# A linear-attention and MLP kernel: chunk 0's output transfers put behind a transposing transfer on the same queue

## The chip, the cores and the metric

The kernel runs on one core of a Trainium2 chip. The core has five instruction streams that run beside each other: TensorE (PE, matrix products; its weight loads are listed as PEld), VectorE (DVE), ScalarE (ACT), GpSimd (POOL) and SyncE (SP). In this kernel SP does no arithmetic; it only begins transfers, one after the other, in the order of its program. POOL begins the loads that change the type from f32 to bf16. Sixteen DMA engines carry the transfers of both.

The metric is device time in microseconds (us), lower is better. Before the change the median of three runs is 286.52 us (286.44 to 286.90).

## The reference

Linear attention (a positive feature map, no softmax) feeds a two-layer MLP whose activation is `h - tanh(h)`. The weight names begin with `moe_`, but there is no routing.

```python
# q, k, v: (8 batches, 8 heads, 576 positions, 64)
phi = lambda x: np.where(x > 0, x, np.exp(x) - 1.0) + 1.0
q_p, k_p = phi(q), phi(k)
kv  = np.einsum('bhsd,bhse->bhde', k_p, v)
z   = np.sum(k_p, axis=2)
num = np.einsum('bhsd,bhde->bhse', q_p, kv)
den = np.einsum('bhsd,bhd->bhs', q_p, z)[..., None] + 1e-06
x   = (num / den).transpose(0, 2, 1, 3).reshape(4608, 512)
h   = x @ w_in                 # 512 x 2048
out = (h - np.tanh(h)) @ w_out # 2048 x 512, f32 result
```

## The kernel before, in words

**Tiles and stages.** The attention is worked per batch `b` (eight batches of 576 rows). The MLP is worked per chunk `c` (nine chunks of 512 rows), so a chunk straddles batches: chunk 2 (rows 1024 to 1535) is made of rows of batches 1 and 2. For each chunk, layer 1 is 64 products (line 430) into PSUM (the accumulators that PE writes), with tanh on ACT (L436, L441) and the subtraction on DVE (L437, L442). Layer 2 is 64 products (L451), whose four results are copied to an SBUF tile `osb` by ACT (L460) and sent to DRAM by SP (L471). Each `osb` is sent as two transfers of 64 rows, so a chunk makes eight.

**What a batch needs.** POOL begins the loads `load_k`, `load_q`, `load_v` (L92); for batch `b` they fill the tiles `kraw`, `qraw` and `v`. ACT and DVE make phi(k) and phi(q) (L136 to L138, tiles `kp`, `qp`). phi(q) has to be turned round (`qT`). For batches 0 and 1 PE does this; from batch 2 on one transfer begun by SP does it (`a_qT_dma`, L155). `qT` then feeds the products of line 337 (denominators, batches 0 to 2) and of lines 273 and 281 (numerators). For batch 2 the reciprocal denominators go to DRAM (`ds`, L366, four small transfers) and come back spread over the partitions (`rdb`, L369, two large ones). Line 401 multiplies the numerators by `rdb` into `xT`, the input of layer 1. Batches 3 and later scale phi(q) before it is turned round and need no `rdb`.

**The order of the work is written by hand.** For each chunk there are lists `s1[fi]` and `s2[s]` of extra work: `s1[fi]` runs after step `fi` of layer 1, `s2[s]` after step `s` of layer 2. Nothing reorders them later: each engine has its instructions in the order in which the Python code issues them. The places that matter here:

- Chunk 0, the last steps of layer 2: steps 12 to 15 finish the four accumulators and call `evac`, each followed at once on SP by its two output transfers. After step 15 the list `s2[15]` runs: the second half of phi(q) of batch 2 (`rest2(qs[1])`), its transposing transfer `a_qT_dma(2)`, and the DVE part of phi(k) of batch 2.
- Chunk 1, `s1[0]`: POOL copies v of batch 2 (`a_vp`, L199), then runs `gate` (L447), a copy of one element of `qT` that lets POOL go on only when the transposing transfer of batch 2 has landed, and then begins the loads of batch 3 (L92). `s1[12]`: the denominators of batch 2 and the trip through `ds` and `rdb`.
- Chunk 1, layer 2: phi of batch 3 (`s2[2]` to `s2[8]`), the numerators of batch 2 and the scaling of line 401 (`s2[12]`), a small product `q_zb` for batch 3 (L221, `s2[14]`). Chunk 2 then starts at line 430 with the columns of `xT` that line 401 wrote.

**Buffers.** `osb` has five buffers, `kraw` and `qraw` one each, `v` and `qT` two. Transfers of SP carry one of eight completion counters in turn, so a transfer also waits until the transfer eight before it has landed.

Of the kernel before, what the change touches and what calls it, by code (L numbers as in the profile page):

```python
# [18 lines left out]
def kernel(  # L19
# [9 lines left out]
    nc = tc.nc  # L29
    B, H, S, D = q.shape  # L30
# [6 lines left out]
    J = S // 64  # L37
# [57 lines left out]
    def load_k(b):  # L95
        k_t[b] = kpool.tile([128, 2, 2, J, D], BF16, name="kraw")
        load(b, k_t[b], k, b == 0)

    def load_q(b):
        q_t[b] = kpool.tile([128, 2, 2, J, D], BF16, name="qraw")  # L100
        load(b, q_t[b], q, b == 0)

    def load_v(b):
        load(b, v_b[b % 2][:, 0:2], v, b < 2)
# [39 lines left out]
    def a_kphi(b, i):  # L144
        phi(b, k_t, kp_t, "kp", i)

    def a_qphi(b, i):
        phi(b, q_t, qp_t, "qp", i)

    def new_qT(b):  # L150
        qT_t[b] = work.tile([128, 2, J, 2, 64], BF16, name="qT")

    def a_qT_dma(b):
        new_qT(b)
        nc.sync.dma_start_transpose(  # L155
            out=qT_t[b].rearrange("p i j g t -> p (i j) (g t)"),
            in_=qp_t[b].rearrange("p i j h d -> p (i j h d)"))
# [29 lines left out]
    def a_kv(b, b0):  # L187

        kz_t[b], vt = kz_c[b % 2], v_b[b % 2]
        kv_mm(b, lambda rs, h, i, j: vt[rs, h:3:2 - h, i, j, :],  # L190
              lambda cs, hg, i: ps_all[cs, b0 + hg, 128 * i:128 * i + 128].rearrange("p (a e) -> p a e", a=2))

    def a_kz(b, b0):
        ps = ps_all[:, b0:b0 + 2, 0:256].rearrange("p g (i e) -> p g i e", i=2)
        nc.vector.tensor_mul(kz_t[b][:, :, :, 64:96], ps[:, :, :, 64:96], mask)
        nc.vector.tensor_copy(kz_t[b][:, :, :, 0:64], ps[:, :, :, 0:64])
# [4 lines left out]
    def kv_cols_mm(b, b0, o):  # L201
        kz_t[b] = kz_c[b % 2]
        kv_mm(b, lambda rs, h, i, j: vp[rs, i, j, h, :],
              lambda cs, hg, i: ps_all[cs, b0 + hg, o + 66 * i:o + 66 * i + 66])
# [64 lines left out]
    def num_mm(b, i, bank_of):  # L269

        kz, qT = kz_t[b], qT_t[b]
        for rs, cs, h, hg in quads():
            nc.tensor.matmul(ps_all[cs, bank_of(h), :].rearrange("p (j t) -> p j t", j=8), kz[rs, hg, i, 0:64],  # L273
                             qT[rs, i, 0:8, hg, :], start=True, stop=True)

    def rest_mm(b, b0, o):

        kz, qT = kz_t[b], qT_t[b]
        for i in range(2):
            for rs, cs, h, hg in quads():  # L280
                nc.tensor.matmul(ps_all[cs, b0 + h, 64 * i + o:64 * i + o + 64], kz[rs, hg, i, 0:64],
                                 qT[rs, i, 8, hg, :], start=True, stop=True)
        return [ps_all[:, b0 + h, o:o + 128].rearrange("p (i t) -> p i t", i=2) for h in range(2)]
# [37 lines left out]
    def scale_rest(b, pss):  # L321
        rdb = rdb_t[b]
        for h, ps in enumerate(pss):
            nc.vector.tensor_mul(
                xT[:, 2 * h:2 * h + 2, S * b + 512:S * b + 576].rearrange("p a (t c) -> p a t c", t=4),
                ps.rearrange("p a (t c) -> p a t c", t=4), rdb[:, 2 * h:2 * h + 2])
# [83 lines left out]
    def new_ns(b):  # L410

        return rpool.tile([128, NP, J, 64], F32, name="ns", tag="rdb")

    def a_spread_pe(b, pairs):

        for n, p in enumerate(pairs):
            for t in range(4):
                r = slice(32 * t, 32 * t + 32)
                nc.tensor.matmul(ps_all[:, 4 + t, 128 * n:128 * n + 128], sel3[r, p].rearrange("p h e -> p (h e)"),
                                 rden_t[b][r, 0:128], start=True, stop=True)  # L420

    def a_scale(b, p, ns, n):
        nc.vector.tensor_mul(
            xT[:, p, S * b:S * b + 512].rearrange("p (j t c) -> p t j c", j=8, t=4),
            ns[:, p, 0:8].rearrange("p j (t c) -> p t j c", t=4),
            ps_all[:, 4:8, 128 * n:128 * n + 128].rearrange("p t (j c) -> p t j c", c=16))
# [22 lines left out]
    def l2mm(gT, o, i, f0, f1):  # L449
        for fi in range(f0, f1):  # L450
            nc.tensor.matmul(o, gT[:, fi, i * 128:(i + 1) * 128], w_out_sb[:, fi, :],  # L451
                             start=(fi == 0), stop=(fi == NF - 1))

    def evac(c, i, o, f0=0, f1=None):
        f1 = DM if f1 is None else f1
        osb = opool.tile([128, DM], F32, name="osb")
        if f0:
            nc.vector.tensor_copy(osb[:, f0:f1], o[:, f0:f1])  # L458
        else:
            nc.scalar.copy(osb[:, f0:f1], o[:, f0:f1])  # L460

        if c == NC - 1 and i == 3:
            nc.sync.dma_start(
                out=out[(B - 1) * S:, f0:f1].rearrange("(p j) m -> p j m", j=J)[:, J - 2:J],
                in_=osb[:, f0:f1])
            return
        for half in range(2):
            b, j = divmod(2 * (4 * c + i) + half, J)
            cuts = [f0, 256, f1] if c == 3 else [f0, f1]
            for a0, a1 in zip(cuts, cuts[1:]):  # L470
                nc.sync.dma_start(  # L471
                    out=out[b * S:(b + 1) * S, a0:a1].rearrange("(p j) m -> p j m", j=J)[:, j, :],
                    in_=osb[64 * half:64 * half + 64, a0:a1])


    nc.vector.memset(zero, 0.0)  # L476
# [20 lines left out]
    for h in range(2):  # L497
        for hg in range(2):
            for i in range(2):
                m = 4 * hg + 2 * h + i  # L500
# [76 lines left out]
    for c in range(NC):  # L577
# [3 lines left out]
        s2 = {i: [] for i in range(16)}  # L581
        if c == 0:
            sub = {}

            def spread1():
                a_spread_pe(1, range(NP))
                for p in range(NP):
                    a_scale(1, p, sub["ns"], p)

            def kv1():  # L590
                a_kv(1, 4)
                pss = rest_mm(0, 4, 256)
                a_kz(1, 4)
                scale_rest(0, pss)

            def num1():
                ns = sub["ns"] = new_ns(1)
                for i in (1, 0):
                    b0 = 4 + 2 * i
                    num_mm(1, i, lambda h: b0 + h)  # L600
                    nc.scalar.copy(ns[:, i::2, 0:8, :].rearrange("p a j t -> p a (j t)"), ps_all[:, b0:b0 + 2, :])

            s1[11].append(lambda: a_kphi(1, 0))
            s1[13].append(lambda: a_kphi(1, 1))
            s2[3].append(lambda: a_qphi(1, 0))
            s2[4].append(lambda: (a_qphi(1, 1), load_q(2), load_k(2), load_v(2)))
            s2[0].append(prepare)
            s2[8].append(lambda: (a_qT_pe(1, 0, Banks([4, 5])), a_qT_pe(1, 1, Banks([6, 7])), kv1()))
            s2[9].append(lambda: (a_den(1, 4), num1(), spread_rest(1), a_split(1)))
            s2[12].append(spread1)  # L610

            qs, ks = [], []

            def exp2(pieces, src, store, name, i):
                pieces.append(phi_pieces(2, src, store, name, i))
                pieces[i][0]()

            def rest2(f):
                f[1]()
                f[2]()  # L620

            def k2(i):
                ks.append(phi_pieces(2, k_t, kp_t, "kp", i))
                ks[i][1]()

            s2[11].append(lambda: exp2(qs, q_t, qp_t, "qp", 0))
            s2[13].append(lambda: (rest2(qs[0]), exp2(qs, q_t, qp_t, "qp", 1)))
            s2[15].append(lambda: (rest2(qs[1]), a_qT_dma(2), k2(0), k2(1)))
        elif n1 < B:
            if c == 1:  # L630
                def kv2():
                    kv_cols_mm(2, 6, 0)
                    pss = rest_mm(1, 6, 256)
                    kz_copy(2, 6, 0)
                    scale_rest(1, pss)

                s1[8].append(kv2)
            if n1 < QS:
                s1[12].append(lambda: (a_den(n1, 6), a_spread(n1)))
            else:  # L640
                if c == 2:
                    s1[2].append(lambda: (q_den(n1, 0, 0), q_den(n1, 0, 1)))
                e = 2 * (c == 2)
                s1[3 + e].append(lambda: q_den(n1, 1, 0))
                s1[5 + e].append(lambda: q_den(n1, 1, 1))
                s1[7 + e].append(lambda: q_scale(n1))
            m = 12 if c == 1 else 9
            s2[m].append(lambda: a_num(n1, n2 if n2 < B else 0))
            if n2 < B:
                s2[m + 2].append(lambda: (q_zb(n2, 4 if c == 1 else 7), q_prod(n2)))  # L650
                if c > 1:
                    s2[15].append(lambda: (q_den(n2, 0, 0), q_den(n2, 0, 1)))
# [46 lines left out]
        for s in range(16):  # L699
# [14 lines left out]
            if c == 0 and g == 2:  # L714
                for n in (2 * i, 2 * i + 1):
                    f = 8 + 2 * (n // 4)
# [37 lines left out]
```

## Time and profile before

| what | value |
|---|---|
| median of three runs | 286.52 us (286.44 to 286.90) |
| profiled execution, its own time | 285.73 us |
| its span | 284.0 us |
| PE busy | 274.4 us (97%) |
| DVE busy | 175.9 us (62%) |
| ACT busy | 145.1 us (51%) |
| POOL busy | 77.4 us (27%) |
| granted TensorE clock | 1.0 throughout |
| bytes moved by DMA | 33.12 MB, mean 117 GB/s |
| output transfers of 128 KB | 62, median 2.5 us to landing |
| transposing transfers | 6, median 4.7 us to landing |

The span is shorter than the time of the same execution by 1.73 us, which lies around it. All moments in the text count from the start of the span. "A <- B" in a list of waits says that A stood idle until B ended. In the list of DMA queues, q0 holds what POOL begins and q1 what SP begins. The DMA share of a window is the mean over the sixteen engines of the time that packets took, and can be above 1.

### The profile page before, as it was taken

What the parts mean: (1) busy time and instruction counts of PE and PEld (TensorE: products, weight loads), DVE (VectorE), ACT (ScalarE), POOL (GpSimd) and SP (SyncE); (2) the same over time, 40 slices, a digit from 0 to 9 for tenths busy, and PEclk for the clock granted to TensorE, in tenths of its full rate; (3) what the DMA queues carried; (4) which work ended last, traced back from release to release, by engine and by line L of the source; (5) the groups of instructions that cost most, each with busy time, mean ns of one, the idle gap of its engine ahead of it and who ended that gap; (6) DMA issues with size and microseconds to landing.
All of it is one profiled execution on the core that took longest, in us unless ns stands there. A gap on an engine that the chain in (4) does not pass through costs nothing.

```text
span 284.0 us, 5064 instructions
## 1 busy us (share of the span) xinstructions
PE 274.4 (97%) x2056; PEld 131.5 (46%) x2084; DVE 175.9 (62%) x283; ACT 145.1 (51%) x176; POOL 77.4 (27%) x69
## 2 busy tenths in 40 slices
PE   7889999999999999999999999999999999999995
PEld 2564454444434454445444444444444444444443
DVE  5859967984679773976397648764770267006600
ACT  3648546945345663666355736663551355126411
POOL 8743030330180536143605360505050000000000
PEclk9999999999999999999999999999999999999999
DMA  6999999869996299147912793151106210230032
GB/s 100 203 206 210 206 206 209 180 109 201 237 254 117 46 187 214 40 79 129 231 47 54 123 228 82 33 120 43 37 12 124 60 37 2 53 79 17 2 73 74
DMA packets 38743, 33.12 MB, mean 117 GB/s; under 512 B 16160, under 2 KB 34624, under 8 KB 38592
## 3 DMA queue, kind: packets, MB, share of 16 engines
q0 software_dynamic: 17504, 18.35, 39.7%
q1 hardware_dynamic: 21216, 14.45, 21.7%
q8 instruction: 16, 0.26, 0.3%
q14 instruction: 7, 0.06, 0.1%
HBM read 38.14 MB, written 9.46 MB: 168 GB/s over the span
## 4 chain that ended last, share of the span: by engine, by line
PE 67%; DMA 20%; issue 4%; DVE 4%; POOL 3%; ACT 2%; SPq 0%; DVEq 0%; POOLq 0%
PE ps_all L430 34%; PE ps_all L451 30%; DMA qraw<-in_q_dram 9%; DMA v<-in_v_dram 8%; DMA out_dram<-osb 2%; DVE qp L138 1%; PE ps_all L273 1%; POOL vp L199 1%; PE ps_all L184 1%; DVE xT L401 1%; ACT e L136 1%; POOL kraw L92 1%; ACT osb L460 1%; DVE r L137 1%; POOL w_out_sb L112 1%
## 5 line engine op out<-in xcount | busy, mean ns | idle before, releaser
L451 PE MATMUL ps_all<-w_out_sb,gT 128*128 128x512 bf16 x543 | 122.4, 379 | 1.6 <-issue 1.1
L430 PE MATMUL ps_all<-xT,w_in_sb 128*128 128x512 bf16 x550 | 122.3, 379 | 1.1 <-DVE xT L401 0.4
L437 DVE TENSOR_TENSOR gT<-ps_all,th 128x1024 bf16<-128x1024 f32 x64 | 77.7, 1217 | 46.1 <-ACT th L436 46.1
L436 ACT ACTIVATE th<-ps_all 128x1024 f32<-128x1024 f32 x64 | 65.7, 1026 | 47.5 <-PE ps_all L430 45.5
L430 PEld LDWEIGHTS <-w_in_sb 128*128 128x128 bf16 x560 | 54.6, 98 | 66.5 <-issue 1.3
L451 PEld LDWEIGHTS <-gT 128*128 128x128 bf16 x560 | 53.9, 98 | 63.4 <-issue 0.2
L460 ACT COPY osb<-ps_all 128x512 f32<-128x512 f32 (+1 forms) x36 | 20.7, 582 | 53.8 <-PE ps_all L451 37.5
L245 POOL TENSOR_TENSOR qp<-qp,rd 128x1152 bf16<-128x1152 bf16 x10 | 21.0, 2118 | 39.8 <-issue 23.7
L231 POOL TENSOR_TENSOR pr<-qp,zb 128x1152 f32<-128x1152 bf16 x10 | 23.5, 2361 | 19.5 <-ACT zb L224 17.0
L136 ACT ACTIVATE e<-qraw 128x1152 bf16<-128x1152 bf16 x16 | 18.5, 1162 | 9.1 <-DMA qraw<-in_q_dram 9.1
L236 DVE TENSOR_REDUCE dn<-pr 128x9 f32<-128x576 f32 x20 | 14.5, 746 | 12.2 <-POOL pr L231 12.2
L136 ACT ACTIVATE e<-kraw 128x1152 bf16<-128x1152 bf16 x15 | 17.5, 1167 | 2.3 <-DMA kraw<-in_k_dram 2.3
L138 DVE TENSOR_TENSOR qp<-e,r 128x1152 bf16<-128x1152 bf16 x16 | 12.1, 758 | 5.0 <-ACT e L136 4.0
L138 DVE TENSOR_TENSOR kp<-e,r 128x1152 bf16<-128x1152 bf16 x15 | 11.7, 783 | 5.0 <-ACT e L136 4.3
L92 POOL DMA_DIRECT2D kraw<-in_k_dram x7 | 5.4, 772 | 27.5 <-ACT e L136 14.1
L442 DVE TENSOR_TENSOR gT<-ps_all,th 128x512 bf16<-128x512 f32 x16 | 10.3, 686 | 2.4 <-ACT th L441 1.7
L441 ACT ACTIVATE th<-ps_all 128x512 f32<-128x512 f32 x16 | 9.2, 598 | 4.9 <-PE ps_all L676 3.7
L92 POOL DMA_DIRECT2D qraw<-in_q_dram x7 | 5.2, 744 | 19.5 <-DVE r L137 12.2
L523 PE MATMUL ps_all<-zero 128*128 128x512 bf16 x31 | 8.7, 433 | 1.3 <-DVE zero L476 1.2
L199 DVE COPY vp<-v 128x1152 bf16<-128x1152 bf16 x10 | 5.2, 524 | 4.0 <-DMA v<-in_v_dram 4.0
L137 DVE TENSOR_SCALAR r<-qraw 128x1152 bf16<-128x1152 bf16 x16 | 7.4, 460 | 0.5 <-DMA qraw<-in_q_dram 0.5
L458 DVE COPY osb<-ps_all 128x128 f32<-128x128 f32 x1 | 0.3, 292 | 11.6 <-DMA out_dram<-osb 11.6
(105 smaller groups left out, 140.5 us busy)
## 6 DMA issues: line engine op xcount, KB each, us to landing
out_dram<-osb SPq DMA_DIRECT2D x62, 128.0 KB, 2.5
kraw<-in_k_dram POOLq DMA_DIRECT2D x7, 576.0 KB, 7.5
qraw<-in_q_dram POOLq DMA_DIRECT2D x7, 576.0 KB, 8.5
v<-in_v_dram POOLq DMA_DIRECT2D x6, 576.0 KB, 11.5
w_in_sb<-in_moe_w_in_dram POOLq DMA_DIRECT2D x3, 512.0 KB, 13.0
w_out_sb<-in_moe_w_out_dram POOLq DMA_DIRECT2D x3, 512.0 KB, 17.3
v<-in_v_dram POOLq DMA_DIRECT2D x4, 288.0 KB, 12.4
rdb<-ds SPq DMA_DIRECT2D x2, 576.0 KB
```

Source lines behind the costliest of these rows:

```text
L92: nc.gpsimd.dma_start(out=t.rearrange("q h i j d -> q (h i) (j d)"), in_=x.rearrange("(n q) x -> q n x", n=4))
L136: return (lambda: nc.scalar.activation(e, x, AF.Exp), lambda: nc.vector.tensor_scalar(r, x, 0.0, 1.0, ALU.max, ALU.add), lambda: nc.vector ...
L138: lambda: nc.vector.tensor_tensor(y, e, r, ALU.min))
L231: nc.gpsimd.tensor_mul(pr_t[b][:, i].rearrange("p j h d -> p j (h d)"), qp_t[b][:, i].rearrange("p j h d -> p j (h d)"), zb_t[b][:, i].uns ...
L236: nc.vector.tensor_reduce(dn_t[b][:, i, :, h], pr_t[b][:, i, :, h, :], mybir.AxisListType.X, ALU.add)
L245: nc.gpsimd.tensor_mul(x, x, rd[:, i].unsqueeze(2).to_broadcast([128, J * 2, D]))
L430: nc.tensor.matmul(h, w_in_sb[:, p, fi * 128:(fi + 1) * 128], xT[:, p, c * 512:(c + 1) * 512], start=(n == 0), stop=(n == NP - 1))
L436: nc.scalar.activation(th, h, AF.Tanh)
L437: nc.vector.tensor_sub(gT[:, fi:fi + 2, :], h, th)
L442: nc.vector.tensor_sub(gT[:, fi, :], h, th)
L451: nc.tensor.matmul(o, gT[:, fi, i * 128:(i + 1) * 128], w_out_sb[:, fi, :], start=(fi == 0), stop=(fi == NF - 1))
L460: nc.scalar.copy(osb[:, f0:f1], o[:, f0:f1])
```

## The change

For chunk 0 `evac` no longer begins its two output transfers; it puts a function that does so into a list `later`. The list is run in `s2[15]` of chunk 0, right behind `a_qT_dma(2)`. The eight transfers themselves (addresses, sizes, order among each other) are the same, and so is everything for chunks 1 to 8. On SP the row of eight output transfers and the transposing transfer of batch 2 change places; the order of the instructions on PE, DVE, ACT and POOL stays as it was. The lines of the changed file lie up to nine higher.

```diff
+    later = []
+
     def evac(c, i, o, f0=0, f1=None):
...
-        for half in range(2):
-            b, j = divmod(2 * (4 * c + i) + half, J)
-            cuts = [f0, 256, f1] if c == 3 else [f0, f1]
-            for a0, a1 in zip(cuts, cuts[1:]):
-                nc.sync.dma_start(
-                    out=out[b * S:(b + 1) * S, a0:a1].rearrange("(p j) m -> p j m", j=J)[:, j, :],
-                    in_=osb[64 * half:64 * half + 64, a0:a1])
+
+        def store():
+            for half in range(2):
+                b, j = divmod(2 * (4 * c + i) + half, J)
+                cuts = [f0, 256, f1] if c == 3 else [f0, f1]
+                for a0, a1 in zip(cuts, cuts[1:]):
+                    nc.sync.dma_start(
+                        out=out[b * S:(b + 1) * S, a0:a1].rearrange("(p j) m -> p j m", j=J)[:, j, :],
+                        in_=osb[64 * half:64 * half + 64, a0:a1])
+
+        if c == 0:
+            later.append(store)
+        else:
+            store()
...
-            s2[15].append(lambda: (rest2(qs[1]), a_qT_dma(2), k2(0), k2(1)))
+            s2[15].append(lambda: (rest2(qs[1]), a_qT_dma(2), [f() for f in later], k2(0), k2(1)))
```

## The prediction

> **What bounds the kernel now.** I read the page's engine shares first, then the chain that ended last, then the instructions of SP, PE and DVE in order of time around the places the change touches, and last the DMA queues window by window.
>
> ```profile
> PE 274.4 (97%) x2056; PEld 131.5 (46%) x2084; DVE 175.9 (62%) x283; ACT 145.1 (51%) x176; POOL 77.4 (27%) x69
> ```
>
> PE is busy nearly always, so only moments at which PE stands still can be won. Those that the change can reach are in this stretch of the chain (start us, length us, what):
>
> ```profile
> 52.34 2.77 POOL vp L199 x2
> 55.11 5.83 issue
> 60.97 0.09 POOL g L447
> ...
> 61.55 0.49 POOL kraw L92
> ...
> 63.01 10.38 DMA v<-in_v_dram
> 73.50 0.46 DVE vp L199
> ...
> 78.98 2.50 DVE xT L401 x4
> 81.52 6.85 PE ps_all L430 x31
> ```
>
> Read it backwards. PE's layer 1 of chunk 2 waited at 81.52 for DVE's scaling; DVE was late because it got v of batch 3 only at 73.50 and from there worked without a gap (5.48 us to line 401); v was late because its load was begun at 63.01; and that because POOL stood at the gate until 60.97. From 81.52 to 266.92 the chain is PE alone. What held the gate is on SP and in the waits:
>
> ```profile
> 50.77 5.24 SPq L471 DMA_DIRECT2D out_dram<-osb  x8
> 56.12 2.92 SPq L155 DMA_TRANSPOSE qT<-qp  x1
> 63.83 1.39 SPq L366 DMA_DIRECT2D ds<-rden  x4
> 70.17 1.12 SPq L369 DMA_DIRECT2D rdb<-ds  x2
> ```
>
> ```profile
> POOL g L447 <- DMA qT<-qp: 5.9, 1, 5.9
> ```
>
> The second half of phi(q) was ready at 51.03 (DVE, line 138, 50.27 + 0.76), but the transposing transfer stood behind eight output transfers until 56.12. What PE lost by this is read from its rows between 77 and 82 us:
>
> ```profile
> 77.66 0.81 PE L451 MATMUL ps_all<-w_out_sb,gT 128*128 128x512 bf16 x3
> 78.72 0.28 PE L221 MATMUL ps_all<-ident,zr 128*128 128x128 bf16 x2 [0.25 <-DVE zr L212]
> 78.84 1.03 PE L451 MATMUL ps_all<-w_out_sb,gT 128*128 128x512 bf16 x4
> 79.73 0.38 PE L430 MATMUL ps_all<-xT,w_in_sb 128*128 128x512 bf16 x1
> 80.32 1.02 PE L430 MATMUL ps_all<-xT,w_in_sb 128*128 128x512 bf16 x4 [0.22 <-DVE xT L401]
> 81.52 0.81 PE L430 MATMUL ps_all<-xT,w_in_sb 128*128 128x512 bf16 x3 [0.17 <-DVE xT L401]
> ```
>
> A product lasts 0.38 us but the next starts 0.21 after it: four take 1.02, and (1.02 - 0.38) / 3 = 0.21. The last of the three at 77.66 starts at 78.09, so L221 could start at 78.30 and starts at 78.72: 0.42 lost. The second L430 could start at 79.94 and starts at 80.32: 0.38. The fifth starts at 80.96; the sixth could follow at 81.17 and starts at 81.52: 0.35. Together 1.15 us; that is all there is to win here.
>
> **The change part by part.**
>
> *The transposing transfer goes ahead of eight output transfers on SP.* SP was free at 50.67 (the `rdb` transfers of line 316 end there), phi(q) is ready at 51.03, the tile's former readers (line 281 for batch 0) were done at 40.6, and its completion counter is now shared with a transfer of line 316 of batch 0, long landed. So it starts at about 51.1, 5.0 us earlier. In the trace it took 4.85 us from its start to the gate (56.12 to 60.97); I take that again, since the load of v of batch 2 leaves the DMA engines at about 52 and the first data came 1.4 us after the start. The gate opens at 51.1 + 4.85 = 55.95. POOL is free for it at 55.11 (end of `vp`). Bounds for this step: 5.0 us earlier, and, were the transfer slowed to twice its 4.85, 0.2 us earlier.
>
> *The output transfers go behind it.* SP is busy 2.92 us with the transposing transfer, to 54.05; then eight at 0.655 (5.24 / 8), to 59.3. The last needs the transposing transfer landed (the counter of eight before), at 55.9, and is issued after 58: no wait. Next on SP are the four `ds` transfers, which wait for `rden` at 63.80 (DVE, 62.75 + 1.05): 4.5 us of cover. ACT needs the `osb` buffers back for chunk 1's second copy at 71.56; with a landing of 7.3 us at the worst the last output transfer is home by 66.6. If that cover were gone it would delay ACT, which has 1.4 us of idle behind it at 74.58. Cost of this part on the path: nothing by itself.
>
> *POOL's loads of batch 3 come earlier* and then run beside output transfers. Before, the three loads had the DMA engines alone:
>
> ```profile
> 59.00:60.00 1.00, 1.00 (x6) 0.43 (x5) 0.54 (x2) 0.52 (x1) 0.00 (x0) 1.00 1.13 217
> 61.00:62.00 1.00, 0.99 (x20) 0.58 (x20) 0.72 (x1) 0.24 (x1) 0.60 (x2) 1.00 0.05 16
> 62.00:63.00 1.00, 1.00 (x7) 0.45 (x5) 0.96 (x3) 0.51 (x1) 1.00 (x2) 1.00 0.01 1
> 70.00:71.00 1.00, 1.00 (x7) 0.47 (x5) 0.00 (x0) 0.79 (x2) 0.00 (x0) 1.00 1.22 210
> ```
>
> (the last two columns are DMA share and GB/s: the engines lay idle from 61 to 63 because of the gate.) Now the loads' first data come at 63.0 - 5.0 = 58.0. The output transfers' data begin 1.3 us after their first issue, at 55.4; 2.6 us at 0.2 MB per us are 0.52 MB of their 1.05 by then, and the other 0.53 MB takes 2.6 us of the loads' time. So v lands 5.0 - 2.6 = 2.4 us earlier, at 71.1. Bounds: 5.0 earlier if the rest of the output does not hold the loads; 0.2 later if all eight (5.2 us) do. I take the middle one, which is the trace's own rate.
>
> *What DVE does with it.* v at 71.1 would put line 401 at 71.1 + 5.48 = 76.6. What is late next is PE: `zr` (L212) reads products of line 184 that end at 76.64, so `zr` 76.7, `kz` 77.05, line 401 from 77.4 to 79.9. PE, without its stalls, has L221 at 78.30, the last four L451 from 78.42, L430 from 79.3, and asks for the last piece of line 401 at its sixth product, 80.4: half a microsecond of cover. All three stalls go. v may land as late as 72.4 before any comes back.
>
> *`rdb` must be there too.* It was no limit before. The queues show its 128 packets of 9216 bytes leaving between 72.0 and 77.15, so it was home at about 77.7; now it must be by 77.9. Its issue waits for `ds`, whose packets stood behind the loads (issued 63.83 to 65.22, moved 67.5 to 69.7). The loads are now done at 70.5, not 72.9, so `ds` is home no later than at 70.1; `rdb` is issued at 70.17, its data start 1.4 us later, at 71.6, take the same 5.15, and are home at 77.3. Bounds: if `ds` comes 2 us sooner, 75.7; if the next load (k of batch 4) takes half the engines, 80.0 (third rival).
>
> That next load was issued 1.37 us after v arrived (74.87); now at 72.5, ready at 74.0. Before, it was ready at about 76.3 but had its first packet at 78.4, when `rdb` was through: the trace lets `rdb` go first, at no cost. The Trainium skill ("DMA: Bandwidth & Descriptors", section "Queues, rings and completion order") says that an engine with work in several queues alternates between them packet by packet. By that rule with equal shares the sum would be +1.0 us and not a gain; by the row it is -1.15. I go by the row, because it shows this pair of transfers.
>
> *Sum:* -0.42 - 0.38 - 0.35 = -1.15 us. Everything from 82 us on is PE's chain; the next meeting with a transfer is `qT` of batch 3, begun at 96.67, home by 101.4 and used at 102.98, so there are 1.6 us of cover, and its own start is paced by PE's layer 1. The profiled execution (285.73, span 284.0) would become 284.6, span 282.85. It lies 0.8 us under the median of 286.52; I apply the same difference to the median: 285.4.
>
> **The rivals.** A kernel like this can be told from no change beyond about 0.2%, 0.57 us.
>
> 1. *Forecast*: all or nearly all stalls of chunk 2's start go, 285.1 to 285.8. 62%.
> 2. *The transfers only change places.* The eight output transfers hold the loads wholly and v lands at 73.3 to 73.7, or `rdb` comes home at 78.5 to 79. For it: the DMA engines are full from 63 to 72 in any order. Against: their idle time at 57 and at 60.4 to 63 now gets used. 286.1 to 286.6. 20%.
> 3. *Slower: k of batch 4 splits the engines with `rdb`.* From 74.0 on `rdb` has 2.75 us to go and would need 5.5: home at 80.0, line 401 at 80.0 instead of 78.98, and PE's sixth product 1.0 later than before: 287.5. It decides as soon as `rdb` lands after 79.0. For it: between 79 and 80 us q0 and q1 both moved packets (136 and 54). Against: the wait to 78.4 told above. 11%.
> 4. *The transfer doesn't start earlier.* The list of waits has one of 2.4 us of line 155 on PE's line 430. If it were real, the gate would stay at 60.97, the outputs would go from 59 to 64.3 into the loads, and v would land up to 5.2 us late: 289 or more. Against: SP was issuing until 56.01, so only 0.1 us was idle. 4%.
>
> The remaining 3% are causes that I don't see.
>
> **How the numbers follow.** The likeliest case gives 285.4, with a range of its own of 285.1 to 285.8. The range of 285.0 to 286.9 takes in cases 1 and 2, some noise, and the mild end of case 3, and leaves out the rest. Faster by over 0.2% (below 285.95): case 1 and the milder half of case 2, 0.71. Within 0.2%: the rest of case 2 and a little of case 3, 0.13. Slower: 0.16.
>
> **What the profile after would show.** The transposing transfer on SP at about 51.1, the outputs from 54.05; POOL's gate at about 56 and the loads from 56.6; v at about 71 and the `vp` copy on DVE there; line 401 at 77.4, idle ahead of it put on PE's products; L221 and the first L430 without a DVE wait. It would be wrong if line 401 still starts near 79 (then look at whether v or `rdb` ended that wait), if the outputs' packets still move after 64 us and hold `ds`, or if a wait appears in chunk 2 or later that takes the 1.15 back.

## The result and the profile after

The changed kernel takes 284.71 us (median of six, 284.22 to 284.85); the kernel before took 286.71 in the same comparison. The ratio is 0.993 with a 95% interval of 0.991 to 0.995: about 2.0 us less. The forecast was 285.4 with a range of 285.0 to 286.9: the direction held, the size did not, and the time lies 0.3 us below the range. A longer comparison later gave the same ratio (0.9929, 0.9903 to 0.9954).

One thing stands out beside the medians. The executions of the changed kernel agree within 0.7 us; those of the kernel before lie anywhere from 284.6 to about 289 us. (Now and then the kernel before also takes 290 to 293 us in a slower state of the chip; the ratios leave those out.)

The profiled execution has a time of 284.85 and a span of 283.0: against the profile of before its time is 0.9 us shorter and its span 1.0, not 2.0. In the chain that ended last PE now holds 80% of the span, against 67% before:

```profile
PE 80%; DMA 13%; POOL 2%; issue 1%; DVE 1%; ACT 1%; SPq 0%; DVEq 0%; POOLq 0%
```

The instructions of SP after the change, in order of time (start us, us). The whole execution is 0.6 us late by 49 us, for a reason that lies ahead of the change; the moments are to be read with that in mind:

```profile
51.71 2.82 SPq L155 DMA_TRANSPOSE qT<-qp  x1
54.64 5.28 SPq L475 DMA_DIRECT2D out_dram<-osb  x8
64.18 1.29 SPq L366 DMA_DIRECT2D ds<-rden  x4
69.28 1.12 SPq L369 DMA_DIRECT2D rdb<-ds  x2
```

The transposing transfer starts 4.4 us earlier and the outputs follow it. `ds` is issued 0.35 us later than before, less than the 0.6 us by which the whole execution is late, and `rdb` 0.9 us earlier. POOL, DVE and PE answer:

```profile
56.43 0.18 POOL L447 COPY g<-qT 1x1 bf16<-1x1 bf16 x1 [0.96 <-DMA qT<-qp]
...
71.22 0.46 DVE L199 COPY vp<-v 128x1152 bf16<-128x1152 bf16 x1 [3.21 <-DMA v<-in_v_dram]
...
77.07 1.67 PE L451 MATMUL ps_all<-w_out_sb,gT 128*128 128x512 bf16 x7 [0.16 <-issue]
77.14 0.42 DVE L212 CAST zr<-ps_all 128x256 bf16<-128x256 f32 x1 [1.11 <-PE ps_all L184]
77.86 2.48 DVE L401 TENSOR_TENSOR xT<-ps_all,rdb 128x512 bf16<-128x512 f32 x4
78.58 0.27 PE L221 MATMUL ps_all<-ident,zr 128*128 128x128 bf16 x2
78.70 1.03 PE L451 MATMUL ps_all<-w_out_sb,gT 128*128 128x512 bf16 x4
79.56 10.74 PE L430 MATMUL ps_all<-xT,w_in_sb 128*128 128x512 bf16 x48
```

DVE has v at 71.22 and now stands idle for 1.11 us ahead of line 212, waiting for PE; PE runs from line 451 through L221 into chunk 2's layer 1 without a wait for DVE. To compare executions I use one stretch throughout, from the first layer-1 product of chunk 1 to the first layer-2 product of chunk 2 ("the stretch"): 45.76 us in the first profile of before (48.49 to 94.25), 44.27 in that of the changed kernel (49.10 to 93.37).

So the steps came as foretold in this pair of profiles, and yet the median moved by 2.0 us where the forecast had about 1.1. The experiments ask where the rest is.

### The profile page after: what moved, and what is told of

It reads as the page before. It is cut to its first block, busy times and chain, and to the rows that moved or that the text cites. A ratio compares the mean times of both kernels' runs of the same rounds, so it can differ in the third digit from the quotient of the medians.

```text
span 283.0 us, 5064 instructions
## 1 busy us (share of the span) xinstructions
PE 274.0 (97%) x2056; PEld 131.6 (46%) x2084; DVE 175.9 (62%) x283; ACT 145.3 (51%) x176; POOL 77.4 (27%) x69
## 4 chain that ended last, share of the span: by engine, by line
PE 80%; DMA 13%; POOL 2%; issue 1%; DVE 1%; ACT 1%; SPq 0%; DVEq 0%; POOLq 0%
PE ps_all L430 39%; PE ps_all L451 37%; DMA qraw<-in_q_dram 7%; DMA w_in_sb<-in_moe_w_in_dram 3%; DMA out_dram<-osb 2%; PE ps_all L184 2%; PE ps_all L273 1%; ACT osb L462 1%; DVE qp L138 1%; POOL v L89 1%; SPq L475 0%; POOL kraw L89 0%; POOL qraw L89 0%; ACT e L136 0%; PE ps_all L337 0%
## 5 line engine op out<-in xcount | busy, mean ns | idle before, releaser
L462 ACT COPY osb<-ps_all 128x512 f32<-128x512 f32 (+1 forms) x36 | 20.7, 582 | 56.4 <-PE ps_all L451 39.3
## 6 DMA issues: line engine op xcount, KB each, us to landing
v<-in_v_dram POOLq DMA_DIRECT2D x4, 288.0 KB, 13.2
```

## The experiments

### Was the first profile of the kernel before a typical one?

The kernel before and the changed one, both unchanged, were run and profiled again.

> The kernel before, once more and unchanged, for a second profile of it. What is open is why the change won 2.0 us where its profiled execution and the sum of stalls have 1.15. Theory (late data): in the kernel before, line 401 hangs on the landing of v with no cover, so every execution in which the loads take longer is longer by as much; the profiled one (285.73) was among the short ones. Then this profile, if its time is near 286.5, has line 401 starting later than the 3.65 us after the first L273 of batch 2 that the first profile shows, by about the excess in time, and PE's loss there is 1.5 to 2 us. Rival (start-up): the executions differ in their first 48 us, where the order of the first loads decides, and PE's loss at chunk 2's start is 1.15 again within 0.2, whatever the time. Time against itself: ratio 1.000 within 0.003.

> The changed kernel, once more and unchanged, timed in more rounds. Theory (late data): -1.6 to -2.2 us against the kernel before, and its own executions agree within 0.7 us, because v has cover now. Rival (start-up, the six executions of before were by chance long ones): -0.9 to -1.4 us. Both: no DVE wait ahead of L221 and the first L430 of chunk 2, line 401 starting 2.2 to 2.3 us after the first L273 of batch 2 (75.61 to 77.86 in the first profile), set by PE's line 184.

Measured: the kernel before against itself 1.0003 (0.9965 to 1.0041), profile 287.32 us; the changed kernel 284.35 us, 0.9929 (0.9903 to 0.9954), profile 284.42. The start-up rival falls: the gain stays at 2 us, and this profile of before has its first layer-1 product of chunk 1 at 48.59, 0.1 us from the first profile's. Ten of the twelve executions of the changed kernel lie within 0.3 us of each other and an eleventh within 0.6, but one took 285.42, so the expected 0.7 us did not hold for all. The stretch is what differs: 47.24 us against 45.76; in the changed kernel 44.28 against 44.27. PE in the second profile of before stands still at a second place too:

```profile
57.37 3.63 PE L430 MATMUL ps_all<-xT,w_in_sb 128*128 128x512 bf16 x16
62.19 0.43 PE L337 MATMUL ps_all<-qT,kz 128*32 128x144 bf16 x16 [1.19 <-DMA qT<-qp]
```

PE itself waited 1.19 us for `qT` ahead of line 337, and POOL's gate opened at 62.10, 6.03 us after the transposing transfer's start and not 4.85. In the first profile `qT` had come just in time: line 337 started 0.08 us after the gate there (60.97 and 61.05), against 0.09 here, and no list showed a wait.

The wait at line 337 looks like a cost of its own, but it is not on the chain that ended last. That chain runs from the gate through the loads, v and DVE, as in the first profile (rows of the second one):

```profile
62.10 0.09 POOL g L447
...
64.15 10.91 DMA v<-in_v_dram
...
75.17 0.46 DVE vp L199
...
80.58 2.48 DVE xT L401 x4
...
83.10 12.89 PE ps_all L430 x59
```

By this chain, had PE not waited at line 337, it would have waited longer at chunk 2's start.

Six more profiles of the kernel before, spread over the study, show how often this happens.

> The kernel before, unchanged, for one more profile. Theory (late transposing transfer): its time goes with the moment at which the gate opens, counted from the start of the transfer: 4.85 us in the execution of 285.73, 6.0 in that with a span of 285.5; PE's wait ahead of line 337 is what the gate's delay is beyond 5.0, and line 401 is later by as much. Rival: the gate opens after 4.85 us and the time differs for another reason.

> The same again, for a fourth profile of the kernel before. Theory (late transposing transfer): if the gate opens within 5 us of the transfer's start the span is 284.0 to 284.4; if it opens later, the span is longer by the excess and up to 0.7 us more. Rival: no such relation.

> The kernel before, a fifth profile. The stretch from the first layer-1 product of chunk 1 to the first layer-2 product of chunk 2 took 45.76, 47.24, 46.30 and 47.10 us in four profiles of it, and 44.27 and 44.28 in two of the changed kernel. Expected: between 45.5 and 47.5, with a PE wait ahead of line 337 if, and only if, the gate opens more than 5 us after the transposing transfer's start.

> The kernel before, a sixth profile, for the link alone. Theory (code load): if the 16 KB packet of the instruction queue near 60 us moves before the transposing transfer's data are through (about 60.4), the gate opens 5.8 to 6.5 us after the transfer's start and PE waits 1.1 to 1.5 us ahead of line 337; if it moves later, the gate opens after 4.75 to 4.9 us and PE waits less than 0.2. Rival (no link): a late gate with a late packet, or the reverse.

> A seventh profile, with the same two expectations: packet inside the data and gate after 5.8 to 6.5 us, or packet after 60.4 and gate after 4.75 to 4.9 us (theory); any other pair (rival).

> An eighth profile, with the same two expectations: packet inside the data and gate after 5.8 to 6.5 us, or packet after 60.4 and gate after 4.75 to 4.9 us (theory); any other pair (rival).

| profile of the kernel before | time, us | gate after the transfer's start | code packet at | PE's wait ahead of L337 | v used by DVE at | the stretch |
|---|---|---|---|---|---|---|
| first | 285.73 | 4.85 | 61.75 | none listed | 73.50 | 45.76 |
| before_again | 287.32 | 6.03 | 59.25 | 1.19 | 75.17 | 47.24 |
| before_p3 | 286.54 | 4.81 | 61.50 | none listed | 74.40 | 46.30 |
| before_p4 | 287.25 | 6.35 | 60.25 | 1.40 | 75.10 | 47.10 |
| before_p5 | 285.78 | 4.81 | 61.75 | none listed | 73.63 | 45.70 |
| before_p6 | 285.47 | 4.84 | 61.75 | none listed | 73.16 | 45.33 |
| before_p7 | 285.29 | 4.82 | 61.25 | none listed | 73.04 | 45.11 |
| before_p8 | 287.10 | 6.36 | 60.00 | 1.37 | 74.74 | 46.92 |

(The moments of the packet are the starts of quarter-microsecond windows.) The time follows the stretch: time less stretch is 240.0 to 240.2 us in all eight. And the stretch follows v: from DVE's copy of v to the first layer-2 product of chunk 2 it is 20.7 to 20.9 us in all eight, with the wait at line 337 or without it. The mean stretch is 46.18 us; the changed kernel's is 44.27. The difference, 1.9 us, is about the measured gain. Most of it is there in every execution: the five in which the transfer landed on time have a mean of 45.64, 1.4 us above the changed kernel. The three in which it landed 1.2 to 1.5 us late have 47.09, and they add the other 0.5 to the mean. Among the on-time ones the loads vary too, and `before_p5` to `before_p8` met what was expected of the gate and line 337. The relation that I expected for before_p3 and before_p4 holds in the second and not in the first, where the gate opened early and v still came late, 13.2 us after the first load's issue instead of 11.9. A row of PE from that profile:

```profile
76.81 0.48 PE L184 MATMUL ps_all<-vp,kp 64*64 64x66 bf16 x36 [0.56 <-DVE vp L199]
```

There even the products of line 184 waited for the copy of v.

Close behind v comes `rdb`. In the shortest of the eight, before_p7, it was `rdb` and not v that released line 401:

```profile
70.35 8.20 DMA rdb<-ds
...
78.64 2.49 DVE xT L401 x4
```

In the first profile the last of the completion counts of `rdb` came at 78.89, again 0.09 us before line 401. By these rows an earlier v with `rdb` unmoved would have won next to nothing in these two executions. In the changed kernel `rdb` is home earlier too (77.3 in after_again).

### Which part of the change wins what?

The changed kernel was given back the late loads, with fills of an unused tile on POOL between the gate and the loads, three in one kernel and five in the other:

```diff
+    hold = const.tile([128, J * 2 * D], BF16, name="hold")
...
-                                  gate(qT_t[n1]), load_k(n2), load_q(n2), load_v(n2)))
+                                  gate(qT_t[n1]), [nc.gpsimd.memset(hold, 0.0) for _ in range(3)], load_k(n2), load_q(n2), load_v(n2)))
```

> The changed kernel, with three fills of an unused tile of 128x1152 (a fill of this size takes 1.08 us at line 489) on POOL between the gate and the loads of batch 3, so that these begin 3.2 us later, at about 60.2. Theory (the DMA engines' backlog counts, not the gate's moment): the chunk 0 outputs have then left the engines when the loads' data begin (61.7), so nothing collides; v lands at about 72.1, 0.9 later than with no fill; DVE has 1.1 us of idle ahead of line 212: no change in time, within 0.3 us of the changed kernel. Rival (each us of delay at the gate is a us for v): v at 74.4, line 401 1.3 to 2 us later, time 1.2 to 1.9 us above the changed kernel.

> The changed kernel with five such fills: the loads begin 5.4 us later, at about 62.4, as late after the rest of the program as in the kernel before; the transposing transfer stays early. If early loads are all that the change wins: v lands at about 74.2, line 401 at about 79.7 instead of 77.9, and the time goes back to that of the kernel before within 0.6 us. Rival (the early transposing transfer itself wins something, at line 337 or by clearing the queue of SP): at least 0.8 us of the gain stays.

Measured against the changed kernel's 284.35 in the same comparison: 285.07 with three fills (0.9956 of before, 0.9933 to 0.9979), 285.94 with five (0.9976, 0.9949 to 1.0002).

| kernel | loads issued | v used by DVE | the stretch | time, us |
|---|---|---|---|---|
| after_again | 56.60 | 71.19 | 44.28 | 284.35 |
| hold3 | 59.35 | 73.16 | 45.14 | 285.07 |
| hold5 | 61.68 | 73.93 | 45.94 | 285.94 |

With three fills, neither side of the expectation held: v came 2.0 us later for 2.75 us of delay, not 0.9 and not 3.2, and 0.7 us of time came back. With five, v is where the kernel before has it, the stalls at chunk 2's start are back, and the result lies between the two sides (the time of before within 0.6 us, or at least 0.8 us of the gain kept): 0.7 us below, by the ratio. PE's rows in the kernel with five fills (its line numbers are one higher than the changed kernel's):

```profile
79.14 0.28 PE L222 MATMUL ps_all<-ident,zr 128*128 128x128 bf16 x2 [0.49 <-DVE zr L213]
79.26 1.03 PE L452 MATMUL ps_all<-w_out_sb,gT 128*128 128x512 bf16 x4
80.12 0.38 PE L431 MATMUL ps_all<-xT,w_in_sb 128*128 128x512 bf16 x1
80.66 1.02 PE L431 MATMUL ps_all<-xT,w_in_sb 128*128 128x512 bf16 x4 [0.16 <-DVE xT L402]
81.86 0.38 PE L431 MATMUL ps_all<-xT,w_in_sb 128*128 128x512 bf16 x1 [0.17 <-DVE xT L402]
```

Two readings. The loss starts where the forecast put it: if each us of v beyond some moment costs one us of the stretch, hold3 puts that moment at 73.16 - 0.86 = 72.3 and hold5 at 73.93 - 1.66 = 72.3, and the forecast said 72.4. And early loads are worth 1.6 us (285.94 - 284.35). Whether the early transposing transfer brings anything beyond them is not shown: hold5 is 0.24% below the kernel before, just within the uncertainty. But its twelve executions lie between 285.59 and 286.38, where the kernel before spreads over 4 us. What the early transfer takes away is the spread.

### Do the outputs cost anything where they stand now?

The kernel before without the eight output transfers of chunk 0 (512 rows of the result are then never written):

```diff
-        for half in range(2):
+        for half in range(2 if c else 0):
```

> The kernel before, with the eight output transfers of chunk 0 left out (512 rows of the output are never written). The transposing transfer starts at 51.1 with nothing ahead of it and nothing behind. Theory (the outputs cost nothing where the change puts them): the same time as the changed kernel, 284.35 within 0.2 us, although v lands 2 to 2.7 us sooner (68.5 to 69.2), because PE no longer waits for it. Rival (the collision of outputs and loads costs the changed kernel part of the gain): 0.4 us or more below it.

And the change for half of them, two of the four tiles:

```diff
-        if c == 0:
+        if c == 0 and i >= 2:
             later.append(store)
```

> Half of the change: the outputs of the first two of chunk 0's four tiles (four transfers) go ahead of the transposing transfer, the other four behind it. It starts at about 53.7 (51.1 + 4 x 0.655). Theory 1 (the kernel before is long and scattered because its transposing transfer lands with no cover ahead of line 337; any cover of more than 2 us takes this away): gate at 58.5, loads from 59.1, v like that of the run with three fills (73.2); time about 285.0 and executions within 1.3 us of each other. Theory 2 (a transposing transfer that runs right behind outputs on the same queue is itself erratic, whatever its place): the executions scatter over 2 us or more, like those of the kernel before (284.6 to 288.9), and the median is above 285.3, since a late gate is a late v.

Without the outputs: 284.59 us (284.19 to 284.92), ratio 0.9928 (0.9897 to 0.9958); v at 69.68, 13.35 us after the gate, against 14.79 and 15.17 in the two profiles of the changed kernel. The outputs hold the loads up by 1.4 to 1.8 us (I had put 2.6), and it costs nothing: the ratio is that of the changed kernel and the stretch is 44.24. With half of them ahead: 284.88 us (284.37 to 285.47), 0.9928 (0.9905 to 0.9952), gate at 58.25, v at 70.65 (the expectation had 73.2), the stretch 44.29. Its executions agree within 1.1 us, so a gate 2.5 us ahead of line 337 and v at 70.65 are early enough. Here line 401 waited 0.29 us for `rdb`, which PE did not feel.

### Does the transposing transfer land late because it runs right behind outputs?

Two kernels. In the first the outputs of chunk 0 are left out and the transfer is held until POOL has copied v, by a tiny transfer ahead of it that reads the copy:

```diff
+    def late():
+        junk = dram.tile([8, 16], BF16, name="junk")
+        nc.sync.dma_start(out=junk, in_=vp[0:8, 1, 0, 0, 0:16])
...
-        for half in range(2):
+        for half in range(2 if c else 0):
...
-            s2[15].append(lambda: (rest2(qs[1]), a_qT_dma(2), k2(0), k2(1)))
+            s2[15].append(lambda: (rest2(qs[1]), k2(0), k2(1)))
...
-            s1[0].append(lambda: (a_vp(2, 0, nc.gpsimd), a_vp(2, 1, nc.gpsimd),
-                                  gate(qT_t[n1]), load_k(n2), load_q(n2), load_v(n2)))
+            s1[0].append(lambda: (a_vp(2, 0, nc.gpsimd), a_vp(2, 1, nc.gpsimd), late(), a_qT_dma(2),
+                                  gate(qT_t[2]), load_k(n2), load_q(n2), load_v(n2)))
```

> The eight output transfers of chunk 0 are left out (512 output rows are not written), and the transposing transfer is held until POOL's copies of v of batch 2 are done (55.1, by one tiny transfer that reads the copy), so that it starts at about 55.7, nearly as late as in the kernel before, but with nothing ahead of it in its queue. Theory (queue): what makes the kernel before scatter is that the transfer runs right behind 1 MB of outputs; here the gate opens 4.85 us after the start, at 60.5, the executions agree within 1.2 us (v still has no cover, so its own scatter shows), and the median is 285.5 to 286. Theory (moment): whatever else happens at 59 to 61 us slows it; here the gate opens after 6 us in about half of the executions, they scatter over 2.5 us or more, and the median is near 286.8.

In the second, SP waits between the outputs and the transfer until the outputs have landed (a tiny transfer overwrites a corner of the last tile sent, `last[0]`):

```diff
+        if c == 0:
+            last[0] = osb
...
-            s2[15].append(lambda: (rest2(qs[1]), a_qT_dma(2), k2(0), k2(1)))
+            s2[15].append(lambda: (rest2(qs[1]), nc.sync.dma_start(out=last[0][63:65, 0:16], in_=q[0, 0, 0:2, 0:16]), a_qT_dma(2), k2(0), k2(1)))
```

> The kernel before with one tiny transfer (2x16 elements into the last tile of outputs, after it has been sent) between the outputs and the transposing transfer: SP waits until the last outputs of chunk 0 have landed, and then begins the transposing transfer at about 58.8, 2.7 us later than in the kernel before. Theory (queue): behind landed outputs it takes its 4.7 us each time, the gate opens at 63.6, PE waits 2.6 us ahead of line 337, the median is about 288.4, but the fast executions agree within 1.2 us. Theory (moment): it scatters as before or the scatter is cut only because the moment has passed; this run alone doesn't tell that apart from the first, the run without outputs does. If the lateness of the gate costs what I hold, each us of it costs one us: 285.7 + 2.7.

The first: 286.27 us, 0.9986 of before (0.995 to 1.0023), executions from 285.03 to 288.62. With no outputs ahead of the transfer the executions still scatter over 3.6 us, where the queue theory allowed 1.2, so that theory falls. Its profile was an undisturbed one (gate after 4.78 us, the stretch 45.32). The second: 288.94 us, 1.0066 (1.0031 to 1.01), executions from 287.51 to 290.24; the transfer started at 57.62, its gate came 4.71 us later, and PE waited 1.23 us ahead of line 337. The executions scatter over 2.7 us, where the queue theory again allowed 1.2. Nothing points at the neighbour in the queue. But neither kernel had a late landing in its one profile, so what scatters in them is not shown; and the profile of the second, 287.51, is its shortest execution, so part of what its median lost was not seen either.

### What makes it late?

In the profiles of before, each late landing goes with one packet. Beside q0 and q1 the trace lists a queue q8 of the kind "instruction" (16 packets and 0.26 MB in the whole span, 16 KB each). One of these packets moves between 58 and 63 us. In before_again it moves in the window from 59.25, and then the transfer's own packets stand still. Its q1 line for the half-microseconds from 59.0, 59.5, 60.0, 60.5 and 61.0 (packets, MB, share of 16 engines):

```profile
q1 hardware_dynamic: 413, 0.11, 112.5%
...
q1 hardware_dynamic: 192, 0.05, 425.0%
...
q1 hardware_dynamic: 7, 0.00, 4.1%
...
q1 hardware_dynamic: 18, 0.00, 8.1%
...
q1 hardware_dynamic: 443, 0.11, 97.7%
```

The 192 packets took far longer than usual (425% of a half-microsecond of the sixteen engines, where 413 packets took 112.5% just before), and over 400 more moved only 1.5 us later. In before_p4 and before_p8 the packet comes at the very end of the data. All but two packets of these are through on time, and the last two move in the windows from 61.0 and 60.75. In the table above all eight pairs agree: packet before 60.5 and late, or packet at 61.25 or after and on time.

To move that packet, the warm-up products at the start were split into two or four narrower ones, which adds instructions and leaves the columns streamed as they were (here the edit with four):

```diff
-            nc.tensor.matmul(ps_all[:, 0, :], zero[:, 0:128], zero, start=True, stop=True)
+            for x in range(4):
+                nc.tensor.matmul(ps_all[:, 0, 128 * x:128 * x + 128], zero[:, 0:128],
+                                 zero[:, 128 * x:128 * x + 128], start=True, stop=True)
```

> The kernel before, with each of the 32 warm-up products of 128x512 at the start split into two of 128x256: the same columns, 32 more products and weight loads, so that TensorE's code from there on lies 64 instructions further on and each 16 KB of code is loaded about 64 instructions earlier in the work. Theory (code load): the time follows where the code load near 60 us falls. If it lies outside the transposing transfer's data (57.4 to 60.3) in the profile, the gate opens within 5 us and the fast executions lie within 1.5 us of each other with a median of 285.4 to 286.2; if inside, the gate opens after 6 us or more and the median is above 287. Rival (no link): scatter and median as in the kernel before (284.6 to 288.9, 286.9), wherever that packet lies.

> The same with each warm-up product split into four of 128x128: 96 more products and weight loads, 192 instructions. The code load near 60 us should come before the 144 instructions of line 184 at 56.5 to 57.3, so before the transposing transfer's data. Theory (code load): gate within 5 us of the transfer's start in every execution, median 285.4 to 286.2 if the start-up stays as long, fast executions within 1.5 us. Rival (no link): scatter of 3 us and a median near 286.9.

> The changed kernel with five fills, whose executions agreed within 0.8 us (285.59 to 286.38, transposing data from 52.6 to 55.4, code load at 58.5), with the warm-up products split into two. Theory (code load): 285.9 and close together as long as no code load falls between 52.6 and 55.4; if the profile has one there, the gate opens 1 to 1.5 us later and the time rises by as much, since v has no cover in this kernel. Rival: 285.9 and close together in any case.

> The same with the warm-up products split into four (192 instructions). The code load is the likelier to fall between 49 and 56. Theory (code load): if it lies inside the transposing transfer's data (52.6 to 55.4), gate at 57 to 57.5 instead of 55.95 and a median of 287 or more; if not, 285.9 as without the split. Rival: 285.9 in any case.

Times: 289.60 (ratio 1.008, 1.0042 to 1.0118), 287.17 (1.0042, 0.9998 to 1.0086), 289.33 (1.0091) and 286.83 (1.0014). As a test of the times this failed: the split made the start longer (the first layer-1 product of chunk 1 at 51.96 in code2 and 49.86 in code4, against 48.6), and the granted clock between 20 and 40 us was 0.93 to 0.95 in all but code4, where it was 1.00. So the four are long, at least in part, for another reason, and their times say nothing about the packet. The pairs are still worth something: code2 has its packet at the end of the transfer's data (63.5) and a gate after 6.46 us; code4 has it after the data (63.0, data through at 61.5) and a gate after 4.81; the two with five fills have no packet inside the data and gates after 4.72 and 4.73. No run breaks the link, one is not clear (settled: packet at 58.25 just ahead of the data, a pause in them from 59.5, landing on time). That the packet causes the pause was not shown; a third cause of both would look the same.

## Why the prediction was wrong

**The mechanism was right.** POOL's gate, the loads behind it, v, DVE's row of work and line 401 are the path, as hold3 and hold5 show from the other side. Gate: forecast 4.85 us after the transfer's start, measured 4.72. v: forecast 71.1, measured 71.22. Line 401: forecast to be set by line 184, and it is, with 1.11 us of idle ahead of line 212. All three stalls of 0.42, 0.38 and 0.35 us are gone. Where the loss starts, 72.4 was forecast and 72.3 measured. That v was met so closely is in part luck: the share of the outputs is 1.4 to 1.8 us and not 2.6, and without any outputs v still took 13.35 us from the gate, 0.8 more than in the first profile of before (12.53), for a reason that no run shows.

**Rivals 2 to 4.** The outputs do not hold the loads wholly (1.4 to 1.8 us, and covered). The transfer does start earlier, so the listed wait of 2.4 us was none. The next load did not split the engines with `rdb`: k of batch 4 was issued at 72.58 and had its first packets at 77, after `rdb`'s last at about 76.2. So the trace's row held, and not equal turns between the queues.

**The step that failed** is the way from the sum to the median: "It lies 0.8 us under the median of 286.52; I apply the same difference to the median". With it falls "Together 1.15 us; that is all there is to win here", which was read from one execution. The forecast for the profiled execution, 284.6, was good: 284.85 and 284.42 were measured. But the 0.8 us did not carry over. In the changed kernel the two profiled executions lie 0.1 us over their medians, because the difference came mostly from when v arrives in the kernel before. I took 4.85 us for the duration of the transposing transfer; it is 4.8 in five and 6.0 to 6.4 in three of eight executions, and the loads vary too. Each us by which v is late costs one us. Over eight and two profiles the stretch shrinks by 1.9 us. Of these, 0.42 is what the first profile lay under the mean of the eight. The first pair alone has 1.49 and not 1.15: 0.13 more lay between lines 184 and 337 (4.50 us against 4.37) and 0.2 in layer 1 before them (8.06 against 7.86). Why the transfer lands late in some executions stays open.

**A reading that was off without harm.** "It was no limit before", of `rdb`: its last count came at 78.89 in the first profile, 0.09 us before line 401 started, and not at about 77.7. So `rdb` was a second limit, nearly as late as v. The forecast for after, 77.3, is what after_again shows.

The hint was on the table: 0.8 us of difference between executions of a kernel whose path runs over uncovered transfers was itself part of what a cover would win. The range ended at 285.0 because it allowed for noise around one execution's sum.

## What to carry to other kernels

A transfer on the path with no cover behind it costs, on average, what its landing varies, and one profile shows one landing only; take several, and price the late landing too. A wait that appears only in the long executions need not be their cost: here the one at line 337 lay off the chain, and the moment of v gave the loss in all eight, within 0.2 us. Look also for the input that came second, within a few tenths of a microsecond of the one that was waited for; it is the next limit. When the profiled execution is shorter than the median, ask which uncovered transfer made the others longer before carrying its sum over. On a queue that starts its transfers in order, what somebody waits for goes ahead of what nobody waits for: here the outputs behind it cost nothing that could be measured.

## What the runs showed of the hardware

- A transposing transfer of this size lands after 4.5 to 4.8 us, or after 6.0 to 6.4. The late landings go with a 16 KB packet of an instruction queue moving during its data, in all of the four late cases (before_again, before_p4, before_p8, code2); the cause is open.
- Outputs that follow a transposing transfer on the same queue did not slow it (4.72 us to the gate with eight behind it); loads that run into those outputs lose 1.4 to 1.8 us over three loads of 576 KB.
- More and narrower warm-up products (the same columns) made the start longer in the kernel before, by the first layer-1 product of chunk 1: 3.4 us with two pieces for each, 1.3 us with four.
